# Expert results kept in the experts' order with a token column; the dense stage scatters its own rows

## The chip, the core and the metric

One core of one Trainium2 chip runs the whole kernel in one launch. The metric is the device time of an execution in microseconds (us), as the median of several runs.

## The reference

Three layers follow one another; 2304 tokens (4 x 576) of 512 features leave the first. `_attn_ref` is attention with rotated queries and keys (8 heads of 64). Then, with `x` as the tokens:

```python
logits = x @ w_gate
expert_idx = np.argmax(logits, axis=1)
...
for e in range(E):
    mask = expert_idx == e
    ...
    xe = x[mask]
    h = np.maximum(xe @ w1[e], 0.0)
    ye = h @ w2[e]
    out[mask] = gate_w[mask, None] * ye
```

with 8 experts of width 1024, and for every token the dense layer, width 2048:

```python
h = x @ w_in
r = np.maximum(h, 0.0)
g = r * r
return (g @ w_out).astype(np.float32)
```

## The kernel before, in words

Attention fills the first 290 us or so and writes its rows to a DRAM table `xd`. `Route` counts the tokens of each expert, gives each expert whole tiles of 128 places (so at most 25 tiles; the last tile of an expert is padded), and puts into `R.idx` for each place the token to fetch (`idx[:, 0]`) and the row to write (`idx[:, 1]`): the token's own row, or for a padded place one of 128 spare rows behind the table (`tokens`, L574 to L584).

`Experts` then walks the tiles in one software pipeline (`run`, L736). Iteration i holds `first(i)` (x times W1, L687), the indirect gather of tile i+2 on POOL (`gather`, L669), the transposes of tile i+1 (L676), `second(i-1)` (h times W2, L709) and `turn_h(i)` (L699). At the end of `second`, DVE scales the tile into the single buffer `yo` (L712), and POOL scatters its 128 rows of 2 KB to the tokens' rows in the DRAM table `yd` (L713). `change` (L716) tests a register: when the next tile belongs to a new expert, ACT, DVE and POOL split the loaded weights in two parts (`split`, L664 and L665) and SP loads the next expert's. 18 iterations stand in the loop; tiles from 18 on are under nested tests (`tail`, L763); here 21 tiles run. `extra(i)` hangs loads and conversions of the dense weights on iterations 0 to 13.

After the last tile, PE runs 26 matmuls on the identity that compute nothing (`keep_warm`, L1015 and L412), and `Dense.run` (L910) follows with 6 blocks of 384 tokens. `load_x` (L852) reads a block of `yd` on SP into `yx`, `turn_x` (L866) transposes it on PE, `first` (L876) and `second` (L897) multiply, two steps of 128 features apart, and `store` (L900) copies three PSUM tiles to SBUF on ACT, DVE, ACT (L905, L907), and SP stores each (L908). Block 0 is loaded at the beginning of `run`, block b+1 at step f = 2 of block b.

Each engine carries out its instructions in the order of the program (the schedule is written out by hand); waits between engines and DMAs are set by the framework from the tiles and DRAM tensors that each instruction reads and writes. The two lines that reach DRAM by token are

```python
nc.gpsimd.indirect_dma_start(out=self.y, out_offset=...(ap=self.R.idx[:, 1, i:i + 1]...), in_=o, in_offset=None)
self.nc.sync.dma_start(out=t[:, c], in_=src[:, c])
```

Of the kernel before, what the change touches and what calls it, by code (L numbers as in the profile page):

```python
# [24 lines left out]
NEXP, FE, FF = 8, 1024, 2048  # L25
NT = 25
# [31 lines left out]
def shape_constants():  # L58

    cols, parts, w = {}, [], 0  # L60

    def add(name, a):
        nonlocal w
        a = np.asarray(a, np.float32).reshape(128, -1)
        cols[name] = (w, w + a.shape[1])
        parts.append(a)
        w += a.shape[1]

    p = np.arange(128)
    half = D // 2  # L70
    inv = 1.0 / 10000.0 ** (np.arange(0, half, dtype=np.float32) / half)
    fr = np.outer(np.arange(S, dtype=np.float32), inv)
    cos, sin = np.cos(fr)[K_AT].T, np.sin(fr)[K_AT].T
    rope = np.stack([np.tile(cos, (4, 1)), np.tile(np.concatenate([-sin, sin]), (2, 1))], 1).astype(np.float32)
    e8 = np.broadcast_to(np.arange(8) - 8, (128, 5, 8))
    add("e8", e8)
    e8n = e8.copy()
    e8n[64:, 4] = 1
    add("e8n", e8n)
    add("U", p[:, None] < p[None, :])  # L80
    add("one", np.ones((128, 128)))
    add("thr", np.broadcast_to(128 * (1 + np.arange(18)), (128, 18)))
    add("thr0", np.broadcast_to(128 * np.arange(18), (128, 18)))
    add("j", np.broadcast_to(p, (128, 128)))
    ids = np.zeros((128, 20))
    for b in range(B):
        for c in range(4):
            ids[:, 5 * b + c] = b * S + 4 * p + c + 1
        ids[:64, 5 * b + 4] = b * S + 512 + p[:64] + 1
    add("ids", ids)  # L90
    e = np.arange(8)
    add("tri", np.broadcast_to(e[:, None] > e[None], (128, 8, 8)))
    add("t", np.broadcast_to(np.arange(NT), (128, NT)))
    add("dump", N + p)

    add("idg", np.where(ids == 0, 1, ids))
    return np.concatenate(parts, 1), cols, rope
# [317 lines left out]
class Route:  # L415
# [107 lines left out]
    def count(self, psum):  # L523
# [7 lines left out]
        v.tensor_reduce(nt, g, axis=AX.X, op=ALU.add)  # L531
        v.tensor_mul(x, self.cst("tri").rearrange("p (a b) -> p a b", b=8), nt.unsqueeze(1).broadcast_to([128, 8, 8]))
# [41 lines left out]
    def tokens(self, wp):  # L574
# [7 lines left out]
        v.tensor_scalar(out=b1, in0=si[:, 0:NT], scalar1=0.5, scalar2=self.cst("dump")[:, 0:1], op0=ALU.is_lt, op1=ALU.mult)  # L582
        v.tensor_add(ind[:, 1], b1, ind[:, 0])
        v.tensor_copy(self.idx[:, 1], ind[:, 1])  # L584

    def control(self, wp):
# [9 lines left out]
        te, ge, ex, q, nx, av, c1 = t("te", 8), t("ge", NT, 8), t("ex", NT), t("q", NT, 8), t("nx", NT), t("av", 8), t("c1", NT)  # L596
        e8 = self.cst("e8")[:, 0:8]
# [17 lines left out]
class Experts:  # L615
# [14 lines left out]
    def buffers(self, wp):  # L630
        self.hh = [wp.tile([128, 2, 8, 128], F32R, name=f"hh{i}") for i in range(2)]
        self.yo = wp.tile([128, 512], F32, name="yo")
# [70 lines left out]
    def second(self, i):  # L703
# [8 lines left out]
        nc.vector.tensor_scalar_mul(o, t, self.R.sg[:, i:i + 1])  # L712
# [98 lines left out]
class Dense:  # L811


    def __init__(self, nc, ident, big, wip, words, wp, ps, y, out, w_in, w_out):
        self.nc, self.ident, self.big, self.words, self.wp, self.ps = nc, ident, big, words, wp, ps
        self.y, self.out, self.w_in, self.w_out = y, out, w_in, w_out
        self.wip = wip
# [34 lines left out]
    def load_x(self, b):  # L852
        t = self.T["y", b] = self.wp.tile([128, 3, 512], F32, name="yx", tag="yx", bufs=1)
        src = self.y[384 * b:384 * b + 384].rearrange("(p c) d -> p c d", c=3)
        for c in range(3) if b == 0 else [slice(0, 3)]:
            self.nc.sync.dma_start(out=t[:, c], in_=src[:, c])  # L856
# [43 lines left out]
    def store(self, b):  # L900
        nc = self.nc
        for c in range(3):
# [5 lines left out]
            nc.sync.dma_start(out=self.out[384 * b:384 * b + 384].rearrange("(p c) d -> p c d", c=3)[:, c], in_=t)  # L908

    def run(self):  # L910
        nb, lag = N // 384, 2
        self.load_x(0)
# [5 lines left out]
        for i in range(16 * nb + lag):  # L918
            b, f = divmod(i, 16)
            if b < nb:  # L920
# [3 lines left out]
                if f == 2 and b + 1 < nb:  # L924
                    self.load_x(b + 1)
                if f in (10, 12, 14) and b + 1 < nb:
# [23 lines left out]
def body(tc, a, cols):  # L950
    nc = tc.nc
    stack = contextlib.ExitStack()
    with stack:
# [3 lines left out]
        yd = dp.tile([N + 128, DM], F32, name="yd")  # L957
# [11 lines left out]
        with tc.manual_schedule():  # L969
# [3 lines left out]
            with tpool("W") as wt, tpool("xg") as xg, tpool("mps", space=PSUM) as ps:  # L973
# [25 lines left out]
                with tpool("mw") as mw:  # L999
# [3 lines left out]
                    def extra(i):  # L1003
# [5 lines left out]
                        if 10 <= i < 14:  # L1009
                            dn.load_out(i - 10)  # L1010
                        if i in (11, 12):
# [32 lines left out]
```

## Time and profile before

| what | value |
|---|---|
| median of 3 runs (lowest to highest) | 1008.9 us (1007.31 to 1009.38) |
| the profiled execution, its own time | 1009.21 us |
| its span in the trace | 1007.4 us |
| busy share of the span: PE, DVE, ACT, POOL | 97%, 53%, 43%, 26% |
| mean granted TensorE clock | 0.988 |
| experts' stage, routing to last scatter | 306 to 586 us |
| dense stage | 592 us to the end |

PE is the matmul engine, PEld its weight loads, DVE, ACT and POOL the vector, scalar and GpSimd engines, SP the engine that issues most DMAs. A "q" behind a name (SPq, POOLq) is that engine's queue of DMA issues, branches and semaphore waits. `L713` is line 713 of the kernel before. The time of an execution holds some 1.8 us that lie outside the span.

### The profile page before, as it was taken

To read this page: it belongs to the slowest core of one execution; us is meant where nothing else is said; L and a number is where in the kernel's file an instruction comes from. 1 tells how busy PE (TensorE), PEld (TensorE's weight loads), DVE (VectorE), ACT (ScalarE), POOL (GpSimd) and SP (SyncE) were. 2 spreads that over 40 slices of the span, in tenths; PEclk is the share of its full clock that TensorE was granted. 3 is DMA by queue.
4 is the path that set the end of the run, shared out by engine and by line. 5 is a ranking of instruction groups with operands and counts; after the bars stand their busy time and mean duration, and the time that the engine had idled before them with its cause. 6 is when DMAs were issued, how large, how long until landed. Compare 5 with 4: busy or idle time off the path is not lost. (4 is left out here: it accounts for less than half of the span.)

```text
span 1007.4 us, 15649 instructions
## 1 busy us (share of the span) xinstructions
PE 973.7 (97%) x5632; PEld 836.6 (83%) x5632; DVE 533.0 (53%) x901; ACT 429.4 (43%) x841; POOL 264.6 (26%) x195
## 2 busy tenths in 40 slices
PE   4999999999997999999999999999999999999998
PEld 3787888787876788888878789999999999999997
DVE  5677777777766355566565449722322323323222
ACT  3666666666632233344455347632222322322222
POOL 3786887796212111123243300000000000000000
PEclk8999999999999899999999999999999999999999
DMA  9876867785354744247365514110010010100000
GB/s 284 235 197 198 233 203 205 226 214 142 98 187 133 239 136 129 85 126 233 127 245 175 186 54 160 40 63 1 1 64 1 12 52 1 63 1 1 32 1 32
DMA packets 43409, 121.21 MB, mean 120 GB/s; under 512 B 5936, under 2 KB 5936, under 8 KB 40880
## 3 DMA queue, kind: packets, MB, share of 16 engines
q1 hardware_dynamic: 38544, 104.95, 33.6%
q0 software_dynamic: 4096, 13.63, 4.1%
q10 hardware_dynamic: 672, 1.44, 0.6%
q8 instruction: 47, 0.77, 0.3%
q14 instruction: 50, 0.41, 0.1%
HBM read 79.90 MB, written 14.94 MB: 94 GB/s over the span
## 5 line engine op out<-in xcount | busy, mean ns | idle before, releaser
L876 PE MATMUL h<-xs,Wi 128*128 128x384 f32 x1152 | 217.3, 337 | 0.7 <-ACT xs L867 0.7
L897 PE MATMUL o<-Wo,gs 128*128 128x512 f32 x864 | 216.0, 394 | 0.0
L876 PEld LDWEIGHTS h<-xs,Wi 128*128 128x128 f32 x1152 | 204.7, 188 | 9.0 <-ACT xs L867 0.9
L897 PEld LDWEIGHTS o<-Wo,gs 128*128 128x128 f32 x864 | 159.9, 188 | 29.3
L885 DVE SCALAR_TENSOR_TENSOR g<-h,r 128x384 f32<-128x384 f32 x80 | 44.6, 558 | 193.0 <-ACT r L881 193.0
L258 ACT ACTIVATE e<-ps,mx 128x576 f32<-128x576 f32 x144 | 106.3, 740 | 82.3 <-DVE mx L251 82.2
L251 DVE TENSOR_REDUCE mx<-ps 128x1 f32<-128x576 f32 x144 | 105.8, 753 | 62.7 <-PE ps L243 62.7
L881 ACT ACTIVATE r<-h 128x384 f32<-128x384 f32 x96 | 47.2, 491 | 212.9 <-PE h L876 212.7
L687 PE MATMUL p_h<-W,xs 128*128 128x512 f32 x504 | 123.2, 400 | 5.3 <-ACTq L720 2.6
L709 PE MATMUL p_y<-W,hh 128*128 128x512 f32 x504 | 121.1, 395 | 2.1 <-DVE W L665 0.9
L687 PEld LDWEIGHTS p_h<-W,xs 128*128 128x128 f32 x504 | 94.7, 192 | 25.8 <-ACTq L720 2.8
L709 PEld LDWEIGHTS p_y<-W,hh 128*128 128x128 f32 x504 | 93.0, 188 | 21.9 <-DVE W L665 1.2
L887 DVE TENSOR_TENSOR gs<-g,gs 128x384 fp32r<-128x384 f32 x96 | 53.5, 558 | 60.1 <-ACT gs L886 60.0
L276 PE MATMUL pp<-ident,e 128*128 128x128 f32 x640 | 85.2, 273 | 0.0
L241 PE MATMUL ps<-kZ,qZ 128*128 128x288 f32 x320 | 78.7, 336 | 6.0 <-DMA qZ<-XL 3.1
L392 POOL TENSOR_TENSOR qk<-qk,TB 128x1280 f32<-128x1280 f32 x28 | 81.4, 2926 | 1.1 <-DMA qk<-in_qk_dram 1.1
L276 PEld LDWEIGHTS pp<-ident,e 128*128 128x128 f32 x640 | 74.9, 141 | 0.5 <-issue 0.4
L886 ACT ACTIVATE gs<-g 128x384 fp32r<-128x384 f32 x96 | 50.5, 526 | 50.5 <-DVE g L885 50.0
L303 PE MATMUL av<-eT,V 128*64 128x288 f32 x512 | 69.1, 412 | 0.0
L241 PEld LDWEIGHTS ps<-kZ,qZ 128*128 128x128 f32 x320 | 49.7, 195 | 22.6 <-ACT X L306 6.1
L292 DVE COPY eT<-pp 128x512 f32<-128x512 f32 x96 | 64.3, 684 | 4.1 <-PE pp L276 2.0
L713 POOL DMA_INDIRECT yd<-yo,idx x21 | 20.9, 993 | 160.1 <-DVE yo L712 153.0
(160 smaller groups left out, 1088.2 us busy)
## 6 DMA issues: line engine op xcount, KB each, us to landing
raw<-in_moe_w_dram SPq DMA_DIRECT2D x44, 512.0 KB, 3.8
qk<-in_qk_dram SPq DMA_DIRECT2D x15, 1280.0 KB, 6.7
kZ<-XH SPq DMA_DIRECT2D x62, 160.0 KB, 2.9
w<-in_moe_w_in_dram SPq DMA_DIRECT2D x8, 1024.0 KB, 5.2
w<-in_moe_w_out_dram SPq DMA_DIRECT2D x8, 1024.0 KB
V<-in_v_dram SPq DMA_DIRECT2D x16, 320.0 KB, 3.3
qZ<-XH SPq DMA_DIRECT2D x31, 160.0 KB, 3.9
qZ<-XL SPq DMA_DIRECT2D x31, 160.0 KB, 2.5
```

The lines of the kernel that those rows point to most:

```text
L241: nc.tensor.matmul(t[:, u, 0:288], Q1[:, qs], K1[:, k0 + 288 * u:k0 + 288 * u + 288], start=i == 0, stop=False)
L251: nc.vector.tensor_reduce(small("mx", P, 9)[:, s:s + 1], T["S", P, s][:, :, 0:288], axis=AX.XY, op=ALU.max, negate=True)
L258: nc.scalar.activation(ed.rearrange("p (u n) -> p u n", u=2), T["S", P, s][:, :, 0:288], AF.Exp, bias=T["mx", P][:, s:s + 1], accum_out=SS ...
L276: nc.tensor.transpose(t[:, c * 128:c * 128 + 128], src, ident)
L292: nc.vector.tensor_copy(o, i)
L303: nc.tensor.matmul(t[64 * j:64 * j + 64], V[:, j, kc], eT[:, j, kc, cs] if kc < 4 else eL[:, cs], start=kc == 0, stop=kc == 4)
L392: v.tensor_tensor(out=out, in0=a, in1=b, op=ALU.mult)
L687: nc.tensor.matmul(t[:, 512 * u:512 * u + 512], s[:, a, k], W1[:, b, k, 512 * u:512 * u + 512], start=n == 0, stop=n == 11)
L709: nc.tensor.matmul(t, s[:, a, k], W2[:, b, k], start=n == 0, stop=n == 23)
L876: nc.tensor.matmul(t, W[:, a, k, fs], s[:, c, k], start=n == 0, stop=n == 11)
L887: nc.vector.tensor_sub(gs[:, 1], g, gs[:, 0].bitcast(F32))
L897: nc.tensor.matmul(self.T["o", b][c], gs[:, a, 128 * c:128 * c + 128], W[:, w], start=(f == 0 and n == 0), stop=(f == 15 and n == 2))
```

## The change

`yd` now keeps each expert's rows together: place 128 t + p of the tile list, less the padding of the experts ahead (`pad`, summed in `tokens`), so the table has no gaps, and padded places still go to the spare rows. Rows are one word wider (`YW` = 513); the last word is the token's number, copied by DVE from `idx[:, 0]` into `yo` before the scatter. Block 0 of `yd` is loaded in iteration 16 of the experts' loop, into a `yx` in a pool that is open there (the first 384 rows come from tiles far ahead of that). In the dense stage POOL copies the three token numbers of a partition out of `yx` (`numbers`), and `store` issues three indirect scatters on POOL to the tokens' rows of the output, where SP stored plain rows.

```diff
--- before.py
+++ after.py
@@ -23,6 +23,7 @@
 N, DM = B * S, H * D
 NPAIR = B * H // 2
 NEXP, FE, FF = 8, 1024, 2048
+YW = 513
 NT = 25
 
 
@@ -92,6 +93,8 @@
     add("tri", np.broadcast_to(e[:, None] > e[None], (128, 8, 8)))
     add("t", np.broadcast_to(np.arange(NT), (128, NT)))
     add("dump", N + p)
+
+    add("place", 128 * np.arange(NT)[None] + p[:, None] - (N + p)[:, None])
 
     add("idg", np.where(ids == 0, 1, ids))
     return np.concatenate(parts, 1), cols, rope
@@ -529,6 +532,9 @@
         nt, tb = self.nt, self.tb
         v.tensor_tensor(out=g, in0=self.bc(cn, 18), in1=self.cst("thr0").unsqueeze(1).broadcast_to([128, 8, 18]), op=ALU.is_gt)
         v.tensor_reduce(nt, g, axis=AX.X, op=ALU.add)
+
+        self.pad = self.p.tile([128, 8], F32, name="pad")
+        v.scalar_tensor_tensor(out=self.pad, in0=nt, scalar=-128.0, in1=cn, op0=ALU.mult, op1=ALU.add)
         v.tensor_mul(x, self.cst("tri").rearrange("p (a b) -> p a b", b=8), nt.unsqueeze(1).broadcast_to([128, 8, 8]))
         v.tensor_reduce(tb[:, 0:8], x, axis=AX.X, op=ALU.add)
 
@@ -579,8 +585,13 @@
         v.tensor_copy(self.idx[:, 0], ind[:, 0])
         yield
 
-        v.tensor_scalar(out=b1, in0=si[:, 0:NT], scalar1=0.5, scalar2=self.cst("dump")[:, 0:1], op0=ALU.is_lt, op1=ALU.mult)
-        v.tensor_add(ind[:, 1], b1, ind[:, 0])
+
+        ge = self.ge
+        v.tensor_mul(ge, ge, self.pad.unsqueeze(1).broadcast_to([128, NT, 8]))
+        v.tensor_reduce(b1, ge, axis=AX.X, op=ALU.add)
+        v.tensor_add(b1, b1, self.cst("place"))
+        v.scalar_tensor_tensor(out=b1, in0=si[:, 0:NT], scalar=0.5, in1=b1, op0=ALU.is_ge, op1=ALU.mult)
+        v.tensor_scalar(out=ind[:, 1], in0=b1, scalar1=self.cst("dump")[:, 0:1], scalar2=None, op0=ALU.add)
         v.tensor_copy(self.idx[:, 1], ind[:, 1])
 
     def control(self, wp):
@@ -593,8 +604,8 @@
             return wp.tile([128, *s], F32, name=n, tag="f" + n, bufs=1)
 
         nt, tb = self.nt, self.tb[:, 0:8]
-        te, ge, ex, q, nx, av, c1 = t("te", 8), t("ge", NT, 8), t("ex", NT), t("q", NT, 8), t("nx", NT), t("av", 8), t("c1", NT)
-        e8 = self.cst("e8")[:, 0:8]
+        te, self.ge, ex, q, nx, av, c1 = t("te", 8), t("ge", NT, 8), t("ex", NT), t("q", NT, 8), t("nx", NT), t("av", 8), t("c1", NT)
+        e8, ge = self.cst("e8")[:, 0:8], self.ge
         plus(v, te, tb, nt)
         compare(v, ge, self.cst("t").unsqueeze(2).broadcast_to([128, NT, 8]), te.unsqueeze(1).broadcast_to([128, NT, 8]), ALU.is_ge)
         v.tensor_reduce(ex, ge, axis=AX.X, op=ALU.add)
@@ -629,7 +640,7 @@
 
     def buffers(self, wp):
         self.hh = [wp.tile([128, 2, 8, 128], F32R, name=f"hh{i}") for i in range(2)]
-        self.yo = wp.tile([128, 512], F32, name="yo")
+        self.yo = wp.tile([128, YW], F32, name="yo")
 
     def num(self, row, i, mn=0, mx=8, engines=None):
         kw = {} if engines is None else dict(engines=engines)
@@ -709,7 +720,8 @@
                 nc.tensor.matmul(t, s[:, a, k], W2[:, b, k], start=n == 0, stop=n == 23)
                 n += 1
         o = self.yo
-        nc.vector.tensor_scalar_mul(o, t, self.R.sg[:, i:i + 1])
+        nc.vector.tensor_scalar_mul(o[:, 0:512], t, self.R.sg[:, i:i + 1])
+        nc.vector.tensor_copy(o[:, 512:513].bitcast(I32), self.R.idx[:, 0, i:i + 1])
         nc.gpsimd.indirect_dma_start(out=self.y, out_offset=bass.IndirectOffsetOnAxis(ap=self.R.idx[:, 1, i:i + 1].bitcast(U32), axis=0),
                                      in_=o, in_offset=None)
 
@@ -814,7 +826,7 @@
     def __init__(self, nc, ident, big, wip, words, wp, ps, y, out, w_in, w_out):
         self.nc, self.ident, self.big, self.words, self.wp, self.ps = nc, ident, big, words, wp, ps
         self.y, self.out, self.w_in, self.w_out = y, out, w_in, w_out
-        self.wip = wip
+        self.wip, self.yxp = wip, words.p
         self.T = {}
 
     def load_in(self, j):
@@ -850,10 +862,13 @@
             nc.vector.tensor_sub(W[:, 1], a, W[:, 0].bitcast(F32))
 
     def load_x(self, b):
-        t = self.T["y", b] = self.wp.tile([128, 3, 512], F32, name="yx", tag="yx", bufs=1)
-        src = self.y[384 * b:384 * b + 384].rearrange("(p c) d -> p c d", c=3)
-        for c in range(3) if b == 0 else [slice(0, 3)]:
-            self.nc.sync.dma_start(out=t[:, c], in_=src[:, c])
+        t = self.T["y", b] = self.yxp.tile([128, 3, YW], F32, name="yx", tag="yx", bufs=1)
+        self.nc.sync.dma_start(out=t, in_=self.y[384 * b:384 * b + 384].rearrange("(p c) d -> p c d", c=3))
+
+    def numbers(self, b):
+
+        t = self.T["to", b] = self.wp.tile([128, 3], I32, name="to", tag="to", bufs=2)
+        self.nc.gpsimd.tensor_copy(t, self.T["y", b][:, :, 512].bitcast(I32))
 
     def turn_x(self, b, c):
         nc = self.nc
@@ -905,11 +920,12 @@
                 nc.vector.tensor_copy(t, self.T["o", b][c])
             else:
                 nc.scalar.activation(t, self.T["o", b][c], AF.Copy)
-            nc.sync.dma_start(out=self.out[384 * b:384 * b + 384].rearrange("(p c) d -> p c d", c=3)[:, c], in_=t)
+            nc.gpsimd.indirect_dma_start(out=self.out, out_offset=bass.IndirectOffsetOnAxis(ap=self.T["to", b][:, c:c + 1].bitcast(U32), axis=0),
+                                         in_=t, in_offset=None)
 
     def run(self):
         nb, lag = N // 384, 2
-        self.load_x(0)
+        self.numbers(0)
         self.split_in(0)
         self.split_out(0)
         self.split_in(1)
@@ -923,6 +939,8 @@
                     self.weights(f)
                 if f == 2 and b + 1 < nb:
                     self.load_x(b + 1)
+                if f == 9 and b + 1 < nb:
+                    self.numbers(b + 1)
                 if f in (10, 12, 14) and b + 1 < nb:
                     self.turn_x(b + 1, f // 2 - 5)
             if i >= lag:
@@ -954,7 +972,7 @@
         pool = lambda name, bufs, **kw: stack.enter_context(tc.tile_pool(name=name, bufs=bufs, **kw))
         pp, dp = pool("p", 1), pool("d", 1, space=DRAM)
         xd = dp.tile([N, DM], F32, name="xd")
-        yd = dp.tile([N + 128, DM], F32, name="yd")
+        yd = dp.tile([N + 128, YW], F32, name="yd")
         ident = pp.tile([128, 128], F32, name="ident")
         make_identity(nc, ident)
         tpool = lambda name, **kw: tc.tile_pool(name=name, bufs=1, reuse_waits="tile", **kw)
@@ -1008,6 +1026,9 @@
                                 dn.convert_in(i - 1)
                         if 10 <= i < 14:
                             dn.load_out(i - 10)
+                        if i == 16:
+
+                            dn.load_x(0)
                         if i in (11, 12):
                             dn.convert_out(i - 11)
```

**The end of the program.** SP in the kernel before, from the load of the last block on (`DMAHW` and `DMASW` with a number are the completion counters of DMAs that SP or ACT, or POOL, issued; a queue takes its eight in turn):

```order
L856 DMA yx<-yd 128x1536 [waits DMAHW0_49,PE_49]
L908 DMA out_dram<-os 128x512 [waits DMAHW5_49,Activation_49]
L908 DMA out_dram<-os 128x512 [waits DMAHW6_49,DVE_49]
L908 DMA out_dram<-os 128x512 [waits DMAHW7_49,Activation_49]
L908 DMA out_dram<-os 128x512 [waits Activation_49]
L908 DMA out_dram<-os 128x512 [waits DMAHW1_49,DVE_49]
L908 DMA out_dram<-os 128x512 [waits DMAHW2_49,Activation_49]
```

POOL in the changed kernel, from the last copy of token numbers (`to`) on:

```order
L871 COPY to<-yx 128x3 [waits DMAHW6_49,DMASW0_49]
L923 DMA out_dram<-os,to 2304x512 [waits Activation_49,Pool_49]
L923 DMA out_dram<-os,to 2304x512 [waits DMASW1_49,DVE_49]
L923 DMA out_dram<-os,to 2304x512 [waits DMASW2_49,Activation_49]
L923 DMA out_dram<-os,to 2304x512 [waits DMASW3_49,Activation_49,Pool_49]
L923 DMA out_dram<-os,to 2304x512 [waits DMASW4_49,DVE_49]
L923 DMA out_dram<-os,to 2304x512 [waits DMASW5_49,Activation_49]
```

The stores moved from SP, where each waits for the copy that fills its buffer and at most for an old counter, to POOL, where each after the first of a block also names the counter of the scatter just ahead of it (1 and 2, then 4 and 5): all scatters name the whole output as their target.

**The row numbers.** DVE before, from the gate's last addition to the first two weight splits of W2 (`ind` and `b` are `tokens`' own tiles, `raw` the loaded weights):

```order
L572 TENSOR_TENSOR sg<-p_t_3587,sg 128x25
L582 TENSOR_SCALAR b_3675<-p_y_3590,consts 128x25
L583 TENSOR_TENSOR ind<-b_3675,ind 128x25
L584 CAST idx<-ind 128x25
L665 TENSOR_TENSOR W_3570<-raw_3575,W_3570 128x1024
```

DVE in the changed kernel, the same stretch:

```order
L578 TENSOR_TENSOR sg<-p_t_3589,sg 128x25
L590 TENSOR_TENSOR ge<-ge,pad 128x200
L591 TENSOR_REDUCE b_3677<-ge 128x25
L592 TENSOR_TENSOR b_3677<-b_3677,consts 128x25
L593 SCALAR_TENSOR_TENSOR b_3677<-p_y_3592,b_3677 128x25
L594 TENSOR_SCALAR ind<-b_3677,consts 128x25
L595 CAST idx<-ind 128x25
L676 TENSOR_TENSOR W_3572<-raw_3577,W_3572 128x1024
```

Two operations of 25 columns became two of 200 and three of 25, ahead of the same weight splits.

**From experts to dense.** PE before, from the keep-warm matmuls on:

```order
L412 MATMUL p_x<-ident 128x128 [waits DVE_49]
L412 MATMUL p_x<-ident 128x128 x25
L866 MATMUL xt<-ident,yx 128x128 [waits DMAHW5_49,PE_49]
L866 MATMUL xt<-ident,yx 128x128 x3
L866 MATMUL xt<-ident,yx 128x128 [waits DMAHW6_49,Activation_49]
L866 MATMUL xt<-ident,yx 128x128 x3
L866 MATMUL xt<-ident,yx 128x128 [waits DMAHW7_49]
```

PE in the changed kernel:

```order
L415 MATMUL p_x<-ident 128x128 [waits DVE_49]
L415 MATMUL p_x<-ident 128x128 x25
L881 MATMUL xt<-ident,yx 128x128 [waits DMAHW5_49,PE_49]
L881 MATMUL xt<-ident,yx 128x128 x3
L881 MATMUL xt<-ident,yx 128x128 [waits Activation_49]
L881 MATMUL xt<-ident,yx 128x128 x7
L891 MATMUL h_7793<-xs,Wi 128x384 [waits DVE_49,Activation_49]
```

SP in the changed kernel, at the end of iteration 16:

```order
L656 DMA raw_3580<-in_moe_w_dram 128x2x512
L732 UNCONDITIONAL_BRANCH x2
L866 DMA yx<-yd 128x1539
L647 TENSOR_LOAD ctl
L647 ISA x2
```

The transposes keep their place behind the 26 matmuls on PE; the load that they wait for moved on SP from behind the last tile to iteration 16, behind that iteration's weight loads.

## Rows read from the trace of the kernel before

**Rows 1.** The page's first line: length of the profiled execution.

```profile
span 1007.4 us, 15649 instructions
```

**Rows 2.** Chain of waits that ended last, 550 to 600 us: start, length, what.

```profile
577.55 3.10 DMA yd<-yo,idx
...
585.63 3.13 DMA yd<-yo,idx
...
588.83 3.36 DMA yx<-yd
```

**Rows 3.** Timeline, 560 to 600 us: start, length, engine, line, operation [idle before, releaser].

```profile
584.60 0.75 DVE L712 TENSOR_SCALAR yo<-p_y,sg 128x512 f32<-128x512 f32 x1 [5.67 <-PE p_y L709]
...
585.59 6.07 PE L412 MATMUL p_x<-ident 128*128 128x128 f32 x52 [1.03 <-DVEq L770]
...
592.29 0.42 PEld L866 LDWEIGHTS xt<-ident,yx 128*128 128x128 f32 x4 [0.82 <-PE p_x L412]
592.32 1.91 PE L866 MATMUL xt<-ident,yx 128*128 128x128 f32 x12 [0.66 <-DMA yx<-yd]
...
592.99 1.88 ACT L867 ACTIVATE xs<-xt 128x512 fp32r<-128x512 f32 x3 [3.60 <-PE xt L866]
...
594.91 5.30 PE L876 MATMUL h<-xs,Wi 128*128 128x384 f32 x29 [0.69 <-ACT xs L867]
```

**Rows 4.** Timeline, the last 8 us.

```profile
1002.06 0.60 ACT L907 ACTIVATE os<-o 128x512 f32<-128x512 f32 x1 [3.10 <-PE o L897]
1002.68 1.69 SPq L908 DMA_DIRECT2D out_dram<-os  x3
```

**Rows 5.** The tile os: its stores, and their time from issue to landing.

```profile
L908 SPq DMA_DIRECT2D out_dram<-os x18: 332/333/401, 667.7 to 1004.0; - x18
...
DMA to landing us min/median/max: 2.0/2.0/2.1
```

**Rows 6.** The tile xg: its gathers' time from issue to landing.

```profile
DMA to landing us min/median/max: 3.3/4.0/7.4
```

**Rows 7.** Timeline, 285 to 360 us: routing and first expert tile.

```profile
307.23 0.37 DVE L398 TENSOR_TENSOR ge<-consts,te 128x200 f32<-128x200 f32 x1
307.63 0.36 DVE L600 TENSOR_REDUCE ex<-ge 128x25 f32<-128x200 f32 x1
307.91 0.16 DVE L601 SCALAR_TENSOR_TENSOR av<-nt,consts 128x8 f32<-128x8 f32 x1
...
321.48 0.24 DVE L582 TENSOR_SCALAR b<-p_y,consts 128x25 f32<-128x25 f32 x1
...
322.06 1.22 DVE L665 TENSOR_TENSOR W<-raw,W 128x1024 fp32r<-128x1024 f32 x1
322.81 2.69 POOL L665 TENSOR_TENSOR W<-raw,W 128x1024 fp32r<-128x1024 f32 x1 [13.48 <-ACT W L664]
323.70 4.01 DVE L665 TENSOR_TENSOR W<-raw,W 128x1024 fp32r<-128x1024 f32 x2 [0.42 <-ACT W L664]
...
328.52 7.29 PE L687 MATMUL p_h<-W,xs 128*128 128x512 f32 x22 [2.01 <-DVEq L720]
...
344.14 1.02 POOL L669 DMA_INDIRECT xg<-xd,idx  x1 [0.30 <-issue]
```

**Rows 8.** Timeline, 495 to 560 us: tiles 14 to 18 of the experts.

```profile
521.77 14.52 SPq L645 DMA_DIRECT2D raw<-in_moe_w_dram  x8
...
521.80 5.51 PE L709 MATMUL p_y<-W,hh 128*128 128x512 f32 x23 [0.90 <-DVE W L665]
...
528.38 0.99 POOL L713 DMA_INDIRECT yd<-yo,idx  x1 [5.78 <-DVE yo L712]
...
540.67 0.99 POOL L713 DMA_INDIRECT yd<-yo,idx  x1 [5.07 <-DVE yo L712]
...
549.87 4.81 SPq L643 DMA_DIRECT2D raw<-in_moe_w_dram  x4
```

**Rows 9.** Busy time of each engine by stretch: length, then busy (instructions).

```profile
600.00:1007.00 407.00, 403.38 (x2049) 365.12 (x2047) 149.66 (x240) 136.13 (x257) 0.00 (x0) 1.00 0.09 32
```

## The prediction

> **What bounds the kernel now.** I read the page's first line [rows 1] for the length, then the busy times by stretch [rows 9]: from 600 us on PE is busy 403.38 of 407.00 us and POOL not at all, so the dense stage is PE's from end to end, and this change can touch the time only at its two ends, besides what it adds ahead of it. Next the chain of waits around the step from experts to dense [rows 2]: the last scatter of `yd`, 3.13 us from its start to its landing, then the load of `yx`, 3.36 us, then the transposes at 592.32. Read alone, the chain says that 6.5 us hang on the trip through DRAM. The timeline of the same stretch [rows 3] says otherwise: PE's 26 keep-warm matmuls start at 585.59 and end at 591.66, and the transposes, which PE takes after them in any case, start at 592.32. Only 0.66 us lie between, and the two rows for that moment name different releasers: the matmul row the load, the weight-load row the keep-warm matmuls. Last the end of the program [rows 4, 5]: ACT's copy of the first output tile ends at 1002.66, and SP's three stores start between 1002.68 and 1004.0 and land 2.0 us after their starts.
>
> **The change, part by part**, against the profiled execution (1009.21 us, 0.31 us above the median of 1008.9).
>
> *A. The padding in `count`:* one DVE operation on 128x8 in the dependent run between attention and the experts. Its like, 128x8 with two inputs, is 0.16 us long [rows 7], partly overlapped with its neighbours. **+0.1 us** (0.05 to 0.16).
>
> *B. The places in `tokens`:* three operations on DVE, 321.48 to 322.06, 0.58 us or 0.19 each, become six. A product of 128x200 costs 0.40 (307.23 to the next start at 307.63), a reduction of 128x200 0.36 plus a gap of 0.03, four small ones 0.19 each, 0.77: 1.56 us, 0.98 more. Behind them on DVE stand three of the four weight splits of W2, and PE waits for DVE to pass them: its first product of tile 1 resumes at 328.52, some 0.8 us after the last split ends at 327.71 [rows 7]. The 0.42 us that DVE then waited for ACT could hide a part. But POOL's split starts at 322.81, and DVE's splits do not run beside it: the first takes 1.22 us, the next two 4.01, 1.57 more than 2 x 1.22, which is most of POOL's stay until 325.50. DVE's first split would now start at 323.04, behind POOL's. From POOL's 322.81, with some 2.2 us for its split alone (323.28 to 325.50) and 3 x 1.22 for DVE's, less the 0.2 us that the two overlapped, the last one ends near 328.5 in place of 327.71. **+0.8 us**, between 0.55 (the 0.42 hides fully) and 0.98. The stalls of PE that I see behind it in the experts' stage are a microsecond or less, so little takes it back.
>
> *C. From experts to dense.* The load of block 0 leaves the path. If it alone ended the wait, transposes, copies and the first product (594.91) move up by 0.66 us; if the keep-warm matmuls did, by nothing. I take the middle, 0.33. DVE's new copy of the token numbers after the last `yo` costs up to 0.1 at the branch that PE's keep-warm run waits for (584.60 plus 0.75 to 585.59). **-0.3 us**, between -0.56 and +0.1.
>
> The load itself goes behind the weight loads of iteration 16 on SP, which end at 536.29 (521.77 plus 14.52), and waits there for the scatter at 528.38 [rows 8]. SP's next work is the weights at 549.87, so 13 us cover it, and without that cover weights would be late. In turn the scatter at 540.67 now waits for that load, and the gather of a later token tile stands behind it on POOL; the gathered rows are used, and `yo` is rewritten, a tile later, and tiles are some 12 us apart (528.38 to 540.67). I cost this at nothing. So too rows of 513 words and 25 more columns of constants.
>
> *E. DVE's copy of 128x1 in each tile* (at most the 0.16 of A) runs while DVE would wait for ACT. Once PE waits for DVE's splits, 521.80, 0.90 us idle [rows 8]; there the copy stands ahead of them. **+0.1 us** (0 to 0.4).
>
> *D. The output.* For the first five blocks three scatters take some 10 us of an otherwise empty POOL in a block of about 68 (407 / 6); their buffers are needed a block later. Nothing. At the end nothing covers them. The two orders shown on the end of the program tell how: SP's stores waited only for their copies, while POOL's second scatter waits for the landing of the first, and the third for the second's. One scatter of 128 rows of 2 KB is 3.10 and 3.13 us from start to landing in quiet stretches [rows 2]; from the end of its wait to its start POOL took 0.28 us (585.35 to 585.63), and between two DMAs of its own 0.30 [rows 7]. So the first starts at 1002.66 + 0.28 = 1002.94, the third 2 x (3.12 + 0.28) = 6.80 later, at 1009.74, and lands at 1012.86. Before, the last store landed at 1004.0 + 2.0, near 1006.04. **+6.8 us.** With no lag between landing and next start, three times 3.10 from 1002.7 make it +6.0. With the gathers' median of 4.0 [rows 6], taken among other traffic, 1002.94 + 2 x 4.28 + 4.0 = 1015.5 make it +9.5. I stay with the scatter rows, the same operation, size and quiet.
>
> The Trainium skill (DMA: Bandwidth & Descriptors, Anatomy of one DMA — SWDGE (gpsimd) path) gives such a DMA 2.0 us fixed, mostly the receipt of the write, plus its bytes at 436 GB/s. By that, my estimate for 262144 bytes is 2.60 us, the last landing comes at 1002.94 + 2 x 2.88 + 2.60 = 1011.30, and the whole at 1014.9. The trace's 3.10 and 3.13 are longer, so they stand.
>
> **Sum:** 0.1 + 0.8 - 0.3 + 0.1 + 6.8 = +7.5 us on 1009.21, which is 1016.7; on the scale of the median, **1016.4 us**. With all low bounds +6.0 (1014.9), with all high ones +11.1 (1020.0).
>
> **Rivals.**
> 1. *The scatters overlap.* The wait might be over when POOL has handed out a scatter's descriptors, not when it lands. Then they start 1.29 us apart (0.99 of issue [rows 8] and 0.30), the third at 1005.52, landing at 1008.64: +2.6 in place of +6.8, 1012.2 us, with bounds from 1011 on. For it: PE, ACT and DVE have no part in it. Against it: POOL's order names the counters, and the SP load at 588.83 waited for just such a counter until 3.13 us after the scatter's start.
> 2. *Not slower: the chain is right at the boundary.* If the 6.5 us of scatter and load all come back, as the chain has it, they pay for the tail: 0.1 + 0.8 + 0.1 + 6.8 - 6.5 = +1.3, about 1010.2 us. It decides if the keep-warm run on PE ends about 5 us sooner, before 587. Against it: in the order shown the 26 matmuls stand ahead of the transposes in both kernels, and they start when the last tile leaves.
> 3. *Scatters to the output land as slowly as gathers do,* 4.0 us: 1019.1. For it, the rows' spread of 3.3 to 7.4 [rows 6]; against it, the quiet end.
>
> That the change does not do what it says, I leave no room for: the orders show each move.
>
> **How the numbers follow.** A measurement of this kernel tells some 0.2%, 2 us, from no change. Forecast 0.79; rival 1 0.07 (0.06 slower, 0.01 within 0.2%); rival 2 0.05 (0.03 within, 0.02 faster); rival 3 0.06; something unseen 0.03, a third each way. Slower 0.79 + 0.06 + 0.06 + 0.01 = 0.92, same 0.01 + 0.03 + 0.01 = 0.05, faster 0.03. The range takes in the forecast's own low end, 1014.9, with a us for the spread of the runs, and rival 3: 1014.0 to 1019.5. Rivals 1 and 2 and the unseen, 0.15, stay out.
>
> **What would show it.** In the changed kernel's profile: three scatters on POOL after the last product, each starting about 3.4 us after the one before, and the span ending that much later; the transposes of block 0 right behind the keep-warm matmuls, with no wait for `yx`; block 0's load on SP near 536 us; DVE's last W2 split about 0.8 us later against its `sg` addition, and PE's resumption with it. I am wrong if the last three scatters start less than 2 us apart, if the dense stage shows PE waiting for POOL or DVE, or if the first product of the dense stage moves up by more than 0.7 us against the last expert product.

## The result, and the profile after

| | before | after |
|---|---|---|
| median (lowest to highest) | 1009.02 us (1007.31 to 1009.38, 4 runs) | 1018.02 us (1017.01 to 1019.31, 4 runs) |
| profiled execution, its span | 1009.21, 1007.4 | 1017.01, 1015.2 |

The ratio is 1.0093, with a 95% interval of 1.0074 to 1.0112: slower. 1016.4 was forecast, 1014.0 to 1019.5.

Cut at events that both kernels have, the two profiled spans differ like this (us; each length is a difference of two starts in the timelines):

| stretch | before | after | difference | forecast |
|---|---|---|---|---|
| start to the first product with W1 | 313.39 | 311.24 | -2.15 | +0.1 (A) |
| to the gate's last addition `sg` | 8.00 | 8.05 | +0.05 | 0 |
| `sg` to PE's resumption with tile 1 | 7.13 | 8.03 | +0.90 | +0.8 (B) |
| to the last `yo` | 256.08 | 255.61 | -0.47 | +0.1 (E) |
| last `yo` to the first dense product | 10.31 | 9.46 | -0.85 | -0.3 (C) |
| to ACT's first copy of the last block | 407.15 | 407.26 | +0.11 | 0 |
| that copy to the end of the span | 5.37 | 15.55 | +10.18 | +6.8 (D) |
| sum | 1007.4 | 1015.2 | +7.8 | +7.5 |

The sum is near; D and C are not, and most of the first row's difference has other causes than A (below). The end of the program, in the timeline of the changed kernel:

```profile
999.65 0.60 ACT L922 ACTIVATE os<-o 128x512 f32<-128x512 f32 x1 [3.21 <-PE o L912]
...
1001.01 0.96 POOL L923 DMA_INDIRECT out_dram<-os,to  x1 [53.95 <-ACT os L922]
...
1004.49 0.96 POOL L923 DMA_INDIRECT out_dram<-os,to  x1 [2.52 <-DMA out_dram<-os,to]
1007.97 0.96 POOL L923 DMA_INDIRECT out_dram<-os,to  x1 [2.52 <-DMA out_dram<-os,to]
```

The chain of waits there ("issue": the engine waited for nothing that the profile shows):

```profile
1001.01 2.71 DMA out_dram<-os,to
...
1003.76 0.73 issue
```

Three scatters, 3.48 us from start to start, where SP's three stores were issued within 1.69 us [rows 4]. The third lands near 1010.7; the span ends 4.5 us later. Before, the last store landed near 1006.04 and the span ended 1.4 us later. What fills the 4.5 us is in the rows of the program's last line (duration in ns, least, median and most, then first and last start), after and then before:

```profile
L1062 POOLq DRAIN  x3: 46/109/6660, 1007.7 to 1015.0; - x3
L1062 SPq DRAIN  x3: 7/7/13, 1011.3 to 1014.7; - x3
```

```profile
L1041 POOLq DRAIN  x3: 46/103/4081, 588.5 to 1007.2; - x3
```

POOL's queue has a long drain there, an instruction of the program's closing: 6.66 us from 1007.7 on, that is from 0.2 us ahead of the last scatter's start until 3.7 us behind its landing. The other queues start their last drains at 1014.7, after it. In the kernel before that drain, 4.08 us long, stood at 588.5, behind the last scatter of `yd`, under the dense stage, and cost nothing.

The step from experts to dense, after (each keep-warm matmul is two rows of the trace, so 26 of them are x52):

```profile
582.93 0.75 DVE L723 TENSOR_SCALAR yo<-p_y,sg 128x512 f32<-128x512 f32 x1 [5.67 <-PE p_y L720]
...
583.94 6.07 PE L415 MATMUL p_x<-ident 128*128 128x128 f32 x52 [1.05 <-DVEq L782]
...
590.07 1.53 PE L881 MATMUL xt<-ident,yx 128*128 128x128 f32 x12
590.76 1.58 ACT L882 ACTIVATE xs<-xt 128x512 fp32r<-128x512 f32 x3 [3.08 <-PE xt L881]
...
592.39 6.52 PE L891 MATMUL h<-xs,Wi 128*128 128x384 f32 x36 [0.79 <-ACT xs L882]
```

The transposes follow the keep-warm matmuls within 0.06 us and wait for no load, where 0.66 us lay between [rows 3]. The load itself left SP early:

```profile
535.28 0.34 SPq L866 DMA_DIRECT2D yx<-yd  x1
```

On POOL the next scatter of `yd` waited 10.52 us for that load and started at 544.23, behind its `yo` 5.2 us later than before; PE shows no wait around it, so the cost that the prediction put at nothing was nothing.

DVE and POOL around the row numbers, after (the same stretch of before is in [rows 7]):

```profile
319.29 0.18 DVE L578 TENSOR_TENSOR sg<-p_t,sg 128x25 f32<-128x25 f32 x1
...
320.71 2.36 POOL L676 TENSOR_TENSOR W<-raw,W 128x1024 fp32r<-128x1024 f32 x1 [12.82 <-ACT W L675]
320.89 2.22 DVE L595 CAST idx<-ind 128x25 int32<-128x25 f32 x1
323.03 3.48 DVE L676 TENSOR_TENSOR W<-raw,W 128x1024 fp32r<-128x1024 f32 x3
...
327.32 2.08 PE L698 MATMUL p_h<-W,xs 128*128 128x512 f32 x4 [2.88 <-DVEq L732]
```

The 2.15 us at the top are not shown to be the change's. Of them 0.74 lie ahead of the routing, in attention: the first keep-warm matmuls of the routing start at 293.22 before and 292.48 after, and in the other profiles of this document, none of which edits attention, anywhere from 292.06 to 295.37. Another 1.54 arise in the next run of keep-warm matmuls. By stretch (length, PE busy, then the other engines, and granted clock third from the end), before and then after:

```profile
300.00:302.00 2.00, 2.00 (x12) 2.00 (x10) 1.93 (x7) 0.00 (x0) 0.00 (x0) 0.50 1.00 368
```

```profile
300.00:302.00 2.00, 2.00 (x22) 2.00 (x20) 1.90 (x8) 0.00 (x0) 0.00 (x0) 1.00 1.04 394
```

Before, the granted clock fell to 0.50, its lower level of 1.2 GHz; in the profiled execution after it stayed at 1.00. The run of 24 matmul rows in the timeline: before, after, and in the run below with the early row numbers, whose code there is that of the changed kernel:

```profile
298.85 4.49 PE L412 MATMUL p_y<-ident 128*128 128x128 f32 x24 [1.36 <-DVE rk L392]
298.18 2.94 PE L415 MATMUL p_y<-ident 128*128 128x128 f32 x24 [1.43 <-DVE rk L395]
298.57 4.52 PE L415 MATMUL p_y<-ident 128*128 128x128 f32 x24 [1.43 <-DVE rk L395]
```

The kernel before with 4 keep-warm matmuls at the other place (below) took 2.94 here. So single spans of either kernel can differ by some 1.5 us for this alone; below, runs are compared by stretches, and by medians over several runs.

### The profile page after: what moved, and what is told of

Same layout as the page of the kernel before. It is cut to its first block, busy times and chain, and to the rows that moved or that the text cites. A ratio compares the mean times of both kernels' runs of the same rounds, so it can differ in the third digit from the quotient of the medians.

```text
span 1015.2 us, 15691 instructions
## 1 busy us (share of the span) xinstructions
PE 969.6 (96%) x5632; PEld 831.4 (82%) x5632; DVE 535.5 (53%) x926; ACT 430.1 (42%) x841; POOL 284.4 (28%) x219
## 5 line engine op out<-in xcount | busy, mean ns | idle before, releaser
L912 PE MATMUL o<-Wo,gs 128*128 128x512 f32 x864 | 218.3, 397 | 0.0
L891 PEld LDWEIGHTS h<-xs,Wi 128*128 128x128 f32 x1152 | 202.2, 188 | 9.3 <-ACT xs L882 1.0
L923 POOL DMA_INDIRECT out_dram<-os,to x18 | 17.4, 968 | 371.1 <-issue 177.8
```

The source lines that it names most:

```text
L891: nc.tensor.matmul(t, W[:, a, k, fs], s[:, c, k], start=n == 0, stop=n == 11)
L912: nc.tensor.matmul(self.T["o", b][c], gs[:, a, 128 * c:128 * c + 128], W[:, w], start=(f == 0 and n == 0), stop=(f == 15 and n == 2))
```

## The experiments

### Where the loss sits: the tail

The tail is the time from the start of ACT's first copy of the last block to the end of the span.

**Last block stored by SP.** In `store`:

```diff
+            if b == 5:
+                nc.sync.dma_start(out=self.out[384 * b:384 * b + 384].rearrange("(p c) d -> p c d", c=3)[:, c], in_=t)
+                continue
             nc.gpsimd.indirect_dma_start(out=self.out, ...
```

> The changed kernel, but the last block is stored by SP as plain rows, so those 384 rows lie in the experts' order in the output (this part of the work is left out). Theory: the whole loss sits behind the last product. From ACT's first copy of the last block to the end of the span the changed kernel took 15.55 us and the kernel before 5.37; this one takes about 5.4, and the time comes back by 10.2 us, to 1006 to 1009 us, the time of before within 2 us. Rival: the 15 scatters of the five blocks ahead, or the wider rows and the row numbers, carry a large part; then the tail shortens to 5.4 all the same but the time stays 2 us or more above before.

Measured: 1008.26 us against 1007.94 of before on the same chip, ratio 1.0001 (0.9991 to 1.0011).

```profile
1001.85 0.60 ACT L922 ACTIVATE os<-o 128x512 f32<-128x512 f32 x1 [3.22 <-PE o L912]
1002.47 1.73 SPq L924 DMA_DIRECT2D out_dram<-os  x3
```

```profile
L1065 POOLq DRAIN  x3: 46/109/6412, 948.1 to 1007.0; - x3
```

The span is 1007.3, the tail 5.45 us. Everything else that the change does, 15 scatters of the output included, adds up to no measurable difference. POOL's drain is as long as ever, 6.41 us, but it stands at 948.1, behind the last scatter of the block ahead, and is covered.

**Three tables.** What keeps the scatters apart, the transfers or the wait?

```diff
-            nc.gpsimd.indirect_dma_start(out=self.out, ...
+            to = self.out if b < 5 or c == 0 else self.spare[c - 1]
+            nc.gpsimd.indirect_dma_start(out=to, ...
...
+        spare = [dp.tile([N, DM], F32, name=f"sp{i}") for i in range(2)]
```

> The changed kernel, but the last block's second and third scatter go to two other DRAM tables (256 rows of the output stay unwritten), so that no scatter names the target of the one ahead. Theory: the wait for the landing of the scatter ahead sets the 3.48 us between starts, not POOL's issue and not the transfers. Then the three start about 1.3 us apart, the third at about 2.6 us behind the first instead of 6.96, and the span ends 7.2 us behind the third start as it does now: the tail from ACT's first copy is 11.2 us instead of 15.55, the time 4.4 us below the changed kernel's, about 1012.8 us. Rival: the transfers themselves queue one behind the other; the starts move together but the landings do not, each later than 2.7 us, and the tail stays above 14 us.

Measured: 1013.99 us, ratio 1.0060 (1.0042 to 1.0077); span 1010.8.

```profile
999.61 0.60 ACT L922 ACTIVATE os<-o 128x512 f32<-128x512 f32 x1 [3.22 <-PE o L912]
...
1000.98 0.96 POOL L924 DMA_INDIRECT out_dram<-os,to  x1 [53.97 <-ACT os L922]
...
1002.24 0.96 POOL L924 DMA_INDIRECT sp<-os,to  x1 [0.30 <-issue]
1003.50 0.96 POOL L924 DMA_INDIRECT sp<-os,to  x1 [0.30 <-issue]
```

Starts 1.26 us apart, and landings of 2.7 us as before, the tail 11.2: as the theory had it to the tenth. By the ratios the time is 3.3 us below the changed kernel's, for the 4.4 expected; the intervals allow both. The wait for the landing, set because each scatter names the whole output, was the 3.48 us. The end is still 7.3 us behind the third start.

**One store of the kernel before through POOL.**

```diff
-            nc.sync.dma_start(out=self.out[...][:, c], in_=t)
+            (nc.gpsimd if b == 5 and c == 2 else nc.sync).dma_start(out=self.out[...][:, c], in_=t)
```

> The kernel before with one edit: of the 18 stores the very last goes through POOL as a plain DMA in place of SP. Theory: the end of the program waits some 4.5 us longer when POOL has put out a DMA shortly before, because POOL drains; the kernel before has that drain hidden under the dense stage. Then the last copy ends as now, the DMA starts 0.73 us later, lands 2.7 us after that, and the span ends 4.5 us behind the landing: the tail from ACT's first copy grows from 5.37 to about 9.9 us, the time by about 4.5 us to 1013.5. Rival: the long closing belongs to the indirect scatters or to the run of three; then the span ends 1.35 us behind the landing and the time grows by 1.4 us only.

Measured: 1010.99 us, ratio 1.0029 (1.0019 to 1.0038), some 2.9 us.

```profile
1001.37 0.60 ACT L907 ACTIVATE os<-o 128x512 f32<-128x512 f32 x1 [3.10 <-PE o L897]
...
1003.62 0.60 POOL L908 DMA_DIRECT2D out_dram<-os  x1 [417.84 <-ACT os L907]
```

```profile
L1041 POOLq DRAIN  x3: 46/115/4713, 1003.6 to 1008.9; - x3
```

The span ends at 1009.1, a tail of 7.7 us. Neither number fits: the drain came and is exposed, against the rival, but it is 4.71 us, not 6.66; the DMA landed after 2.3 us and started 0.30 behind the copy, not 0.73; and the span ends 3.2 us behind the landing, between the theory's 4.5 and the rival's 1.35. So a single DMA on POOL near the end lengthens it, in a kernel without any of the change.

**A small DMA on POOL.** To the kernel with the last block stored by SP, one DMA on POOL is added behind the first copy:

```diff
+                if c == 0:
+                    nc.gpsimd.indirect_dma_start(out=self.spare, ..., in_=t[:, 0:16], in_offset=None)
```

> The kernel of the run with the last block stored by SP as plain rows (rows of that block in the experts' order), plus one small scatter on POOL of 128 rows of 16 words to a spare table, behind ACT's first copy of the last block. Theory: what POOL keeps the end of the program waiting for is a time after a scatter, whatever its size. Then the small scatter starts 1.4 us behind the start of that copy, the span ends near 7 us behind that start, and the tail from the copy's start grows from 5.45 to 7.9 to 8.6 us. Rival: the closing goes with the bytes moved or with the three scatters in a row; a 32nd of the bytes leaves the tail below 6 us.

Measured: 1012.36 us, ratio 1.0042 (1.0026 to 1.0059), against 1.0001 without it.

```profile
1002.63 0.60 ACT L922 ACTIVATE os<-o 128x512 f32<-128x512 f32 x1 [3.22 <-PE o L912]
...
1003.99 0.96 POOL L926 DMA_INDIRECT sp<-os,to  x1 [53.96 <-ACT os L922]
```

```profile
L1069 POOLq DRAIN  x3: 46/109/6492, 1003.8 to 1010.8; - x3
```

Span 1011.1, tail 8.5 us: a 32nd of the bytes, and the end still 7.1 us behind the start and, as the DMA lands after 2.5 us, 4.6 behind the landing. Neither the bytes nor the run of three make the closing.

With `nc.gpsimd.dma_start(out=self.spare[0:128], in_=t[:, 0:16])` in its place:

> The same with a plain DMA of 128 rows of 16 words on POOL in place of the small scatter. Theory: plain DMAs on POOL close sooner, as with the last store of the kernel before put on POOL, where the span ended 5.5 us behind the start and 3.2 behind the landing. Then it starts 0.9 us behind the start of the copy and the tail is 6.2 to 6.6 us. Rival: bytes decide, and the tail is 5.5 as without it; or plain and indirect differ in nothing but size, and the tail is as long as with the small scatter, within 0.6 us.

Measured: 1009.99 us, ratio 1.0024 (1.0015 to 1.0034); span 1008.2.

```profile
1000.59 0.60 ACT L922 ACTIVATE os<-o 128x512 f32<-128x512 f32 x1 [3.22 <-PE o L912]
...
1001.48 0.59 POOL L926 DMA_DIRECT2D sp<-os  x1 [53.48 <-ACT os L922]
```

```profile
L1068 POOLq DRAIN  x3: 46/109/5930, 1001.5 to 1007.9; - x3
```

The tail is 7.6, longer than the theory's 6.2 to 6.6, and 0.8 shorter than with the small scatter, where the second rival allowed 0.6: none of them fits. The end comes 6.7 us behind the start, where the large plain DMA of the kernel before had 5.5. But the DMA starts 0.89 us behind the start of the copy, against 1.36 for the small scatter, and lands after 2.2 us, against 2.5. From the landing to the end it is 4.5 us, as behind every scatter at the end. So neither the bytes nor plain against indirect changes the closing. The 3.2 us of the kernel before, where POOL had been idle for 417.84 us, stand alone; why they are shorter stays open.

**Two of three scatters under PE's work.** The last block's second products are reordered; the later steps' `gs` live in word buffers that are free by then:

```diff
...
+                if b2 == nb - 1 and f2 >= 10:
+                    if f2 == 15:
+                        for c in range(3):
+                            for g in range(10, 16):
+                                self.second(b2, g, (c,))
+                            self.store(b2, (c,))
+                    continue
                 self.second(b2, f2)
...
```

> The changed kernel with the last block's second products put in another order: the last six steps are kept back and then done tile by tile (18 matmuls for the first tile, 18 for the second, 18 for the third), so that the first two tiles are done some 7.7 and 3.8 us ahead of the third. The arithmetic is the same. Theory: two of the three serial scatters go under PE's work. The third starts about 0.7 us after its copy, the span ends 7.2 us after that start, so from the last matmul to the end 8.6 us instead of some 14.3; the time falls by 5 to 6 us, to about 1012. Rival: the closing of 7.2 us grows with the number of scatters put out shortly before, or PE stalls for its operands in the new order; then the time falls by less than 4 us.

Measured: 1012.29 us, ratio 1.0042 (1.0027 to 1.0058), 5 us below the changed kernel's 1.0093.

```profile
993.65 0.96 POOL L929 DMA_INDIRECT out_dram<-os,to  x1 [46.88 <-ACT os L928]
...
997.43 0.96 POOL L929 DMA_INDIRECT out_dram<-os,to  x1 [2.82 <-DVE os L926]
...
998.37 2.24 PE L918 MATMUL o<-Wo,w 128*128 128x512 f32 x9
1000.64 0.60 ACT L928 ACTIVATE os<-o 128x512 f32<-128x512 f32 x1 [7.76 <-PE o L918]
1001.51 0.96 POOL L929 DMA_INDIRECT out_dram<-os,to  x1 [3.12 <-ACT os L928]
```

Only the third scatter is left behind PE. The span ends at 1008.8, 8.2 us after the last matmul at 1000.61.

### The step from experts to dense

**4 keep-warm matmuls, in the changed kernel and in the kernel before.**

```diff
-                    keep_warm(nc, ident, X.p_x[:, 0], 26)
+                    keep_warm(nc, ident, X.p_x[:, 0], 4)
```

> The changed kernel with 4 keep-warm matmuls between experts and dense in place of 26. Theory: with the early load the transposes stand behind the keep-warm run alone, so they now start near 1 us behind it, some 5 us sooner. Next in line are ACT's four weight splits, which end at 587.67 in the changed kernel and stand ahead of the copies of the transposed tokens, so the first product of the dense stage starts near 589.4 instead of 592.39 there: from the last yo to it 6.5 us instead of 9.46, and the time falls by 2.5 to 3 us. Rival: PE's idle time lowers its granted clock, and the dense stage gives the gain back over its first microseconds; then the granted clock of 590 to 600 us is well below 1 and the time falls by less than 1 us.

> The kernel before with 4 keep-warm matmuls in place of 26. Theory: there the last scatter and the load of block 0 (3.13 and 3.36 us) are the limit as soon as the keep-warm run is short, so the transposes still start near 592.3 and nothing is gained: from the last yo to the first product 10.3 us as before, and the time within 0.5 us, or later by up to 3 us if the idle PE is granted a lower clock behind it. Rival: the load was not the limit and the time falls by 2 us or more, as in the changed kernel with 4.

The changed kernel: 1018.55 us, ratio 1.0097 (1.0074 to 1.0120), by the median no better than with 26. Its timeline, and one stretch (granted clock third from the end):

```profile
584.98 0.75 DVE L723 TENSOR_SCALAR yo<-p_y,sg 128x512 f32<-128x512 f32 x1 [5.64 <-PE p_y L720]
...
591.23 8.22 PE L891 MATMUL h<-xs,Wi 128*128 128x384 f32 x36 [2.50 <-ACT xs L882]
599.29 2.27 PE L912 MATMUL o<-Wo,gs 128*128 128x512 f32 x9
```

```profile
592.00:594.00 2.00, 2.00 (x9) 1.62 (x8) 1.13 (x2) 0.00 (x0) 0.00 (x0) 0.57 0.00 0
```

The first product comes 6.25 us behind the last `yo`, 3.2 sooner, as expected. But PE was idle for 2.50 us right ahead of it, the granted clock was then 0.57 over 2 us, most of them at its lower level of 1.2 GHz, and 0.58 over the next 2, and the first 36 products took 8.22 us in place of 6.52. Half of the gain was gone eight microseconds later: from the last `yo` to the first `o` product 14.31 us (584.98 to 599.29) against 15.81 (582.93 to 598.74). The other 1.5 us stay: to ACT's first copy of the last block it is 415.21 us against 416.72. The median hides them, in part because the four executions of this run hold 1.95 to 2.83 us outside the span, where all other runs hold 1.7 to 1.9; why is not shown.

The kernel before: 1009.98 us, ratio 1.0024 (1.0013 to 1.0035).

```profile
583.73 0.75 DVE L712 TENSOR_SCALAR yo<-p_y,sg 128x512 f32<-128x512 f32 x1 [5.67 <-PE p_y L709]
...
591.20 2.95 PE L866 MATMUL xt<-ident,yx 128*128 128x128 f32 x12 [5.32 <-DMA yx<-yd]
...
594.84 8.44 PE L876 MATMUL h<-xs,Wi 128*128 128x384 f32 x36 [0.69 <-ACT xs L867]
```

With the short run the chain of scatter and load is the limit, 7.47 us from `yo` to the transposes against 7.72 with the long one, and the clock (0.50 from 592 to 598 us) makes it worse. So the 26 matmuls filled a wait that was there, and kept the clock up for what follows.

**8 keep-warm matmuls, and the transposes ahead of three splits.**

```diff
         self.split_in(0)
+        for c in range(3):
+            self.turn_x(0, c)
         self.split_out(0)
         self.split_in(1)
-        for c in range(3):
-            self.turn_x(0, c)
...
-                    keep_warm(nc, ident, X.p_x[:, 0], 26)
+                    keep_warm(nc, ident, X.p_x[:, 0], 8)
```

> The changed kernel with 8 keep-warm matmuls in place of 26 and the transposes and copies of block 0 put ahead of three of the first four weight splits. Theory: now neither the keep-warm run nor the splits are in front: transposes near 585.9, ACT's copies right behind its first weight split, the first product near 588.2; from the last yo to it 5 to 5.5 us instead of 9.46, the time 3.5 to 4.5 us below the changed kernel's. Rival: the splits that moved back are late for the steps that use them, or the granted clock falls, and less than half of that remains by the end.

Measured: 1013.42 us, ratio 1.0056 (1.0035 to 1.0078), 3.7 us below the changed kernel's ratio.

```profile
583.49 0.75 DVE L723 TENSOR_SCALAR yo<-p_y,sg 128x512 f32<-128x512 f32 x1 [5.67 <-PE p_y L720]
...
588.92 6.51 PE L891 MATMUL h<-xs,Wi 128*128 128x384 f32 x36 [0.79 <-ACT xs L882]
```

```profile
592.00:594.00 2.00, 2.00 (x13) 2.00 (x12) 1.15 (x3) 1.97 (x4) 0.00 (x0) 1.00 0.00 0
```

5.43 us from the last `yo`, and the clock stays at 1.00. The whole gain stays: to ACT's first copy of the last block it is 412.67 us against 416.72.

### The row numbers, and all three together

```diff
                     X.first(0)
+                    next(tokens, None)
                     X.turn_x(1)
                     R.gated()
-                    next(tokens, None)
```

> The changed kernel, but the row numbers are worked out between the first tile's product and the transposes of the second, ahead of the gate's addition, where DVE was idle for 3.37 us waiting for ACT. Theory: they were paid in full, 0.90 us more between the gate's addition and PE's resumption than before (8.03 against 7.13). Moved into the idle stretch they cost nothing, and the old three operations' 0.58 us go too: that distance falls to 6.5 to 7.1 us, and the time by 0.9 to 1.5 us against the changed kernel. Rival: POOL's own split, which holds DVE up, decides when DVE gets past the splits; the distance stays near 8 us and the time the same within its spread.

Measured: 1017.74 us, ratio 1.0091 (1.0074 to 1.0108).

```profile
321.25 0.17 DVE L578 TENSOR_TENSOR sg<-p_t,sg 128x25 f32<-128x25 f32 x1
...
321.67 1.23 DVE L676 TENSOR_TENSOR W<-raw,W 128x1024 fp32r<-128x1024 f32 x1 [0.24 <-ACT W L675]
...
328.14 7.16 PE L698 MATMUL p_h<-W,xs 128*128 128x512 f32 x21 [1.76 <-DVEq L732]
```

The distance fell to 6.89 us, as expected, 1.14 less. The medians cannot show it: their intervals are wider than a microsecond.

The three edits in one kernel:

> The changed kernel with the three edits together: row numbers ahead of the second tile's transposes, 8 keep-warm matmuls with block 0's transposes ahead of three weight splits, and the last block's second products tile by tile. Theory: the three places are apart, so the gains add up: 6.9 us between the gate's addition and PE's resumption, 5.4 from the last yo to the first dense product, 8.2 from the last matmul to the end, each as in the run of that edit alone. Against the kernel before that is -4.9 at the boundary (10.31 to 5.4), -0.2 at the row numbers (7.13 to 6.9) and +4.1 at the end (4.05 to 8.2), so 1 us below it: a ratio of 0.997 to 1.001. Rival: the gains do not add up (PE's granted clock falls, or a later stage gives them back); then one of the three distances is longer than alone and the ratio stays above 1.002.

Measured: 1006.94 us against 1007.88 on the same chip, ratio 0.9991 (0.9981 to 1.0002); span 1004.3. The three distances are 6.88 (319.28 to 326.16), 5.44 (582.22 to 587.66) and 8.13 us (996.17 to 1004.3), so the gains add up and pay for the new tail; whether it beats the kernel before by its one microsecond the interval leaves open.

## Why the prediction was right, and where it was not

The total held because errors of both signs met: D was 3.4 us too small, C 0.55 too small a gain, some 0.5 us went in the experts' stage, and the profiled run had 2.15 us of luck ahead of it, 1.54 of them with the clock. Of the 0.5 us, 0.29 lie in tile 1, where PE's 22 matmuls behind the wait took 7.01 us for 7.29 [rows 7]; the rest, about 0.01 us a tile, has no cause shown. By the medians, +9.0 us were measured for +7.5.

**A** holds: the new `pad` operation moved the next one's start by 0.08 us.

**B** holds in size, +0.90 for +0.8, and in kind: POOL's split went ahead and DVE's three came behind it, in 3.48 us. Unforeseen is that the last small operation, the CAST of 128x25, was caught too, 2.22 us where the same one on `idx` otherwise takes 0.18; in the run with the last block on SP it was 2.21 again. The Trainium skill (SBUF — State Buffer, SBUF: two separate sides) describes a port pair that DVE and GpSimd lock against each other for a whole instruction, and the CAST's end 0.04 us after POOL's agrees; which operations of DVE take that pair no run here sets apart. That it was idle time that they could be moved into, and not a law of these operations, the early row numbers show.

**C** is the step by which, in its own words, I would be wrong: the first product moved up by more than 0.7 us. The wait for the load went whole, 0.60 us, where I took half; and I had not seen that three loads landing one after another also stretched what follows. PE's 12 transposes fell from 1.91 to 1.53 us and ACT's three copies from 1.88 to 1.58.

**E** shows at its place: PE's wait for DVE's splits grew from 0.90 [rows 8] to 1.01 us. In the stretch as a whole it is lost.

```profile
520.21 5.48 PE L720 MATMUL p_y<-W,hh 128*128 128x512 f32 x23 [1.01 <-DVE W L676]
```

**D** is the term that was mis-sized. The chain of three is right: 3.48 us from start to start for my 3.40, though made up otherwise, 2.71 of landing (for 3.12) and 0.77 from there to the next start, 0.73 of it POOL's issue (for 0.28). The first start came 0.76 us behind ACT's copy, not 0.28; in the reordered last block the third started 0.27 behind its copy (1001.24 to 1001.51), so what the 0.76 is made of stays open. The Trainium skill (DMA: Bandwidth & Descriptors, Anatomy of one DMA — SWDGE (gpsimd) path) gave an estimate of 2.60 for the landing, and the measured 2.71 lies nearer to it than the rows of `yd`. The large error is the closing, which I carried over from before, "and the span ending that much later": 4.5 us behind the landing in place of 1.4. I looked for what would cover the scatters and not for what covered POOL's drain; its row at 588.5 stood in the trace of the kernel before.

**Rival 1**, overlapping scatters, is what happens once the targets differ, 1.26 us apart, and does not while they share one. **Rival 2** had a true core: of the 6.5 us on the chain 4.9 can be had (10.31 to 5.43), but not by the early load alone. Behind the load stood the keep-warm run, behind that three weight splits on ACT, and behind them the clock. **Rival 3** does not occur at the end, where landings took 2.7 us.

## What to carry to other kernels

Before moving the last DMAs to another queue, look for that queue's closing work (its drain) and for what covers it now; here its exposure alone cost 3.1 us (4.5 behind the landing for 1.4), more than a scatter takes to land. The scatters waited for each other here because they name one tensor, so give the early ones work to hide under, rather than issuing them together at the end. A run of keep-warm matmuls can hide a wait: shortening one pays only when the load, the engines behind it and the granted clock have all been seen to.

## What the runs showed of the hardware

- The span ended 4.5 to 4.6 us behind the landing of POOL's last DMA in the changed kernel and in every variant of it with such a DMA at the end: 128 rows of 512 words or of 16, indirect or plain, three in a row or one alone. In the kernel before with one plain store on POOL it was 3.2 us, behind SP's last store 1.4. POOL's drain ended 3.7 us behind that landing in those variants; it lasted from 4.08 us in the kernel before to 8.27 with three tables, where it began at 1001.7, ahead of the second scatter.
- An idle stretch of PE of 2.50 us between two stages was followed by a granted clock of 0.57 and 0.58 over 4 us, and the 1.7 us that the next 36 matmuls then took longer (8.22 against 6.52) were half of what the shorter keep-warm run had gained.
- A DVE CAST of 128x25 took 2.22 us beside a POOL addition of 2.36 us, and 0.18 us where POOL was idle.
